# Batch 0 of an attention-and-MLP kernel: the last 64 queries taken out of the score tiles and finished inside the first GEMM, with v and w_in loaded in another order

## The chip, the core and the metric

The kernel runs on one core of a Trainium2 chip. The metric is the device time of one execution in microseconds (us), as the median of several runs. TensorE (PE) does the matrix products, ScalarE (ACT) the exponentials, the Gelus and some copies, VectorE (DVE) copies, products and divisions, GpSimd (POOL) masks, some products and the DMAs that change type, SyncE (SP) only issues DMAs.

## The reference

Eight batches of eight heads, 576 tokens and head width 64 go through causal attention with a forgetting gate; the result, with the heads side by side, is 4608 rows of 512, which go through a two-layer MLP with the exact Gelu.

```python
# q, k, v: (8, 8, 576, 64); f: (8, 8, 576); w_in: (512, 2048); w_out: (2048, 512)
cum = np.cumsum(np.log(np.clip(f, 1e-4, 1.0)), axis=-1)
scores = scale * q @ k^T + cum[:, :, :, None] - cum[:, :, None, :]
scores = np.where(causal, -1e9, scores)          # causal: key after query
x = softmax(scores) @ v                          # then (batch, token, head * 64)
out = gelu(x @ w_in) @ w_out                     # exact Gelu, by erf
```

## The kernel before

The order of all instructions on each engine is the order in which the program writes them; the engines wait for each other with semaphores that a layer adds from the tiles that are read and written. Two heads are a pair `i` (0 to 3). A part of the decay that belongs to the key is put into v as a weight: `weigh_v` multiplies v by `wT` into `vw`, whose last column holds the weight itself, so one product gives numerator and denominator; `normalize` divides.

**Batch 0** is `first_attention` (L577). `load_qk_tokens` loads q and k on POOL's queue two heads at a time. `transposes_first` turns them on PE and copies them to `qT` and `kT`, on DVE except for half of pair 0. `scores` (L279) makes the scores of a pair in four tiles of 896, 768, 896 and 640 columns for the two heads, keys on partitions, each followed by one exponential on ACT (L309). In batch 0 the mask is added by small matmuls (`key_of`, `after`). `attend` (L323) multiplies by `vw` in five blocks of 128 queries; the last block starts at query 448, so its upper 64 queries are the last 64 of the batch. `to_xT` (L356) turns x on PE in five blocks, with the copy on ACT or DVE.

The **first GEMM** (`gemm1`, L380) makes blocks of 128 of the 2048 hidden columns (`ffb` 0 to 15) for the first 512 tokens of a batch. Each block is four matmuls of 512 columns (`kt` 0 to 3, one for each pair) and then a Gelu on ACT. Batch 0 does blocks 0 to 9 in its own stage; 10 to 15 are held until batch 1. The last 64 tokens of each batch go to `tails` by `x_tail` (on POOL) and are multiplied together at the end of the kernel.

`gemm1_begin` (L662) starts the first GEMM while the last pairs are still being turned. Blocks 0 and 1 use the two `m` banks; 2 and 3 are the two halves of one `s` tile (`more`), and their Gelus come after both:

```python
        gemm1(b, 2, (2, 3), pss[2], False)
        gemm1(b, 3, range(4), pss[3], False)
        gelu(b, 2, pss[2])
        gelu(b, 3, pss[3])
```

PSUM has two tiles each of `s` (two banks), `o` and `m` (one bank each).

**Loads.** v of batch 0 comes in pieces of 128 keys by four heads: three on SP's queue (blocks 0 to 2 of the first four heads), seven on POOL's. `w_in` is four pieces of 512 hidden columns on POOL's queue, the first three right behind v, the fourth behind half of batch 1's q, k and v. POOL executes `weigh_v` for pairs 2 and 3 of batch 0 between these issues; at most eight DMAs of a queue are under way, since their semaphores are used in turn. `load_v(0, ...)` is at L154 to L159, `load_w_in` at L627 to L635.

Of the kernel before, what the change touches and what calls it, by code (L numbers as in the profile page):

```python
# [9 lines left out]
FP32 = mybir.dt.float32  # L10
# [5 lines left out]
P = 128  # L16
# [37 lines left out]
def kernel(  # L54
# [95 lines left out]
    diagonal(key_of, Alu.not_equal, 1.0, D)  # L150
    ident_bf = key_of[:, D : D + P]
    load_qk_tokens(0, 4, 6)
    nc.gpsimd.memset(v_sb[:, :, 0, 0:1], 0.0)
    load_v(0, 0, 4, ns=range(3))  # L154
    diagonal(after, Alu.is_ge, -1.0e9, D)
    load_qk_tokens(0, 6, 8)
    diagonal(ident_fp, Alu.not_equal, 1.0, 0)
    load_v(0, 0, 4, nc.gpsimd, range(3, NBLK))
    load_v(0, 4, 8, nc.gpsimd)  # L159

    qT = [consts.tile([P, S], BF16, name=f"qT{i}") for i in range(HP)]
    kT = [consts.tile([P, S], BF16, name=f"kT{i}") for i in range(HP)]
# [6 lines left out]
    def load_w_in(c):  # L169
        f4 = slice(c * d_ff // 4, (c + 1) * d_ff // 4)  # L170
        nc.gpsimd.dma_start(w_in_sb[:, :, f4], w_in_r[:, :, f4])
# [28 lines left out]
    tails = consts.tile([P, n_dm, TC], BF16)  # L200


    def transposes_first(b, i, which, pool, tag):

        src = qk_of[b][which]
        ps = pool.tile([P, JT, PT], BF16, tag=tag, name="ps_f")
        for j in range(JT):
            for h in range(2):
                nc.tensor.transpose(  # L209
                    ps[h * D : (h + 1) * D, j, :],  # L210
                    src[:, 2 * i + h, j * D : (j + 1) * D],
                    ident_bf[:PT, :PT],
                )

        dst = (qT, kT)[which][i].rearrange("d (p j) -> d p j", j=JT)
        src = ps.rearrange("d j p -> d p j")
        if b or i:
            nc.vector.tensor_copy(dst, src)  # L218
        else:
            nc.vector.tensor_copy(dst[:, 0 : PT // 2], src[:, 0 : PT // 2])  # L220
            nc.scalar.copy(dst[:, PT // 2 :], src[:, PT // 2 :])
# [55 lines left out]
    e_of = {}  # L277

    def scores(b, i, t):  # L279
        on_pe = b == 0 or (b == 1 and i == 0)  # L280
        st = s_psum.tile([P, 2, 512], FP32, tag="s", name=f"s{t}")
        c = 0
        for n, q0, w in STILES[t]:
            z = D if n == NBLK - 1 else 0
            masked = on_pe and c in SDIAG[t]
            for half in range(-1, 2 if masked else 0):
                if half == 0 and z:
                    continue
                for h in range(2):
                    d = slice(h * D, (h + 1) * D)  # L290
                    if half < 0:
                        to = st[:, h, c + z : c + w]
                        ab = kT[i][d, K0[n] : K0[n] + P], qT[i][d, q0 + z : q0 + w]
                    else:
                        last = (half + 1) * D
                        to = st[:, h, c + z : c + last]
                        c0 = (1 + h - half) * D
                        ab = key_of[d, c0 : c0 + P], after[d, c0 + z : c0 + last]
                    nc.tensor.matmul(  # L299
                        to, *ab, start=half < 0, stop=half == 1 or not masked  # L300
                    )
            c += w
        z = D if t == 1 else 0
        if z:
            et = e4[(b * HP + i) % len(e4)]
        else:
            et = e_pool.tile([P, 2, 512], BF16, tag=f"e{t}", name=f"e{t}")
        e_of[b, i, t] = et
        nc.scalar.activation(et[:, :, z:c], st[:, :, z:c], Act.Exp, scale=scale)  # L309
        for c0 in [] if on_pe else SDIAG[t]:  # L310
            nc.gpsimd.affine_select(  # L311
                out=et[:, :, c0 + z : c0 + P],
                in_=et[:, :, c0 + z : c0 + P],
                compare_op=Alu.is_ge,
                fill=0.0,
                base=z,
                pattern=[[0, 2], [1, P - z]],
                channel_multiplier=-1,
            )
# [252 lines left out]
    def behind(t, h):  # L572

        g = x_pool.tile([P, 1], FP32, tag="gate", name="gate")
        nc.gpsimd.tensor_copy(g[:PT], t[:, h, 0:1])

    def first_attention():  # L577


        def transposes(i, pool, tag):  # L580
            transposes_first(0, i, 0, pool, tag)
            transposes_first(0, i, 1, pool, tag)

        def attend_head(i, h, *at):
            attend(0, i, h, (0, 1, 2, 3, 4), *at)
            normalize(0, i, h)

        warm_up(9)
        transposes(0, o_psum, "o")
        nc.vector.tensor_tensor_scan(  # L590
            decay[:, S - 2 :: -1],
            f_sb[:, S - 1 : 0 : -1],
            none[:, 0 : S - 1],
            2.0**80,
            Alu.mult,
            Alu.add,
        )
        warm_up(2, 2 * P)
        scores(0, 0, 0)
        scores(0, 0, 1)  # L600
        transposes_first(0, 1, 0, m_psum, "m")
        scores(0, 0, 2)
        transposes_first(0, 1, 1, m_psum, "m")
        psw = o_psum.tile([P, NBLK, BH], FP32, tag="o", name="psw")
        for n in range(NBLK):
            nc.tensor.transpose(
                psw[:, n, :], decay[:, K0[n] : K0[n] + P], ident_fp[:BH, :BH]
            )
        scores(0, 0, 3)
        nc.vector.tensor_copy(wT[:, 0:4, :], psw[:, 0:4, :])  # L610
        nc.vector.tensor_copy(wT[D:P, 4, :], psw[D:P, 4, :])
        nc.vector.tensor_copy(
            vw(0)[:, :, :, D], wT[:, :, 0:H].rearrange("p n h -> p h n")
        )
        scores(0, 1, 0)
        transposes_first(0, 2, 0, m_psum, "m")
        scores(0, 1, 1)
        transposes_first(0, 2, 1, m_psum, "m")
        scores(0, 1, 2)
        scores(0, 1, 3)  # L620
        transposes_first(0, 3, 0, m_psum, "m")
        scores(0, 2, 0)
        transposes_first(0, 3, 1, m_psum, "m")
        weigh_v(0, 0, nc.vector, 0, NBLK - 1)
        weigh_v(0, 0, nc.vector, NBLK - 1)
        weigh_v(0, 1, nc.vector)
        load_w_in(0)  # L627
        load_w_in(1)
        load_w_in(2)
        weigh_v(0, 2)  # L630
        weigh_v(0, 3)
        load_qk_tokens(1, 0, 4)
        nc.gpsimd.memset(v_sb[:, :, 0, 0:1], 0.0)
        load_v(1, 0, 4, nc.gpsimd)
        load_w_in(3)  # L635
        load_qk_tokens(1, 4, 8)
        load_v(1, 4, 8, nc.gpsimd)
        scores(0, 2, 1)
        scores(0, 2, 2)
        scores(0, 2, 3)  # L640
        for ms in ((0, 1, 2, 3), (4,)):
            for h in range(2):
                attend(0, 0, h, ms)
        for h in range(2):
            normalize(0, 0, h)
        scores(0, 3, 0)
        scores(0, 3, 1)
        for h in range(2):
            attend_head(1, h, m_psum, "m")
        scores(0, 3, 2)  # L650
        scores(0, 3, 3)
        for h in range(2):
            attend_head(2, h)
        to_xT(0, 0, nc.scalar.copy)
        to_xT(0, 1, nc.scalar.copy)
        attend_head(3, 0)
        attend_head(3, 1)
        both = s_psum.tile([P, 2, 1024], BF16, tag="s", name="ps_x2")
        to_xT(0, 2, nc.scalar.copy, ps=both[:, 0, 0:XC])
        gemm1_begin(0, both)  # L660

    def gemm1_begin(b, both):  # L662

# [141 lines left out]
    for b in range(B):  # L805
        if b == 0:
            first_attention()
        elif b == 1:
            second_attention()
        else:  # L810
            attention(b)
        if b == 0:
            x_tail(0)
        for ffb in range(4 if b < 2 else 5, n_ff):
            if b == 0 and ffb in HELD:
                continue
            aside = ffb in (7, 8) if b > 1 else b == 1 and ffb % 4 < 2
            gemm1(b, ffb, ps=spare() if aside else None)
            if b == 1 and ffb % 2 == 0:
                at = HELD[(ffb - 4) // 2]  # L820
                gelu(0, at, h_of[at])
            if b == 0:
                if ffb == 7:
                    weigh_v(1, 0)
                    load_w_out(0)
                    weigh_v(1, 1)
                    load_w_out(1)
                    load_qk_tokens(2)
                if ffb == 8:
                    for which in range(2):  # L830
                        transposes_first(1, 0, which, o_psum, "o")
            elif b + 1 < B:
                first, gap = (5, 3) if b == 1 else (1, 4)
                at, late = divmod(ffb - first, gap)
                if late == 0:
                    untangle(b + 1, at)
                if late == gap - 2 and (b > 1 or at < 2):
                    weigh_v(b + 1, at)
                if ffb == (9 if b == 1 else 14):
                    load_qk_tokens(b + 2)  # L840
# [34 lines left out]
```

## Time and profile before

| what | value |
| --- | --- |
| median of 3 runs (lowest, highest) | 336.46 us (335.54, 336.92) |
| the profiled execution, its time | 335.98 us |
| its span, from first to last instruction | 334.1 us |
| granted TensorE clock | 0.999 |
| PE busy | 325.7 us, 97% |
| ACT busy | 206.7 us, 62% |
| first matmul of the first GEMM of batch 0 | 22.89 us |
| first scores of batch 1 | 33.18 us |

Times within the profile are us from the start of the span. In a timeline line the columns are start, length, engine, line, operation, out<-in, shape and count; in brackets stand the idle time of the engine before it and who ended it. In a group line the first number after the bar is busy time, then the mean ns of one instruction, then idle time before them and its releasers. Matmuls are pipelined, so the length of a matmul's line includes its way through the array.

### The profile page before, as it was taken

How to read it: one execution, taken by the hardware profiler on the slowest of the kernel's cores; microseconds unless marked ns; L12 is line 12 of the kernel's file. 1: busy time of each engine (PE TensorE's matmuls, PEld its weight loads, DVE VectorE, ACT ScalarE, POOL GpSimd, SP SyncE). 2: the span in 40 equal slices, each digit the busy share in tenths (PEclk: the TensorE clock that was granted, in tenths of full speed). 3: DMA queues.
4: the chain of work that ended last, by engine and by line, in shares of the span. 5: the costliest groups of instructions: out<-in, count | busy, mean ns of one | idle time of the engine just before them, and what ended most of it. 6: DMA issues, size and time to landing. Idle time of an engine off the chain costs nothing.

```text
span 334.1 us, 7820 instructions
## 1 busy us (share of the span) xinstructions
PE 325.7 (97%) x3161; PEld 170.7 (51%) x3161; DVE 183.9 (55%) x424; ACT 206.7 (62%) x299; POOL 133.3 (40%) x260
## 2 busy tenths in 40 slices
PE   7899999999999999999999999999999999999995
PEld 3674555445554466445644565455544654444443
DVE  5761657754549754894589447954795450010011
ACT  3976886974536786578736892788278836404600
POOL 8897873066336044704453355334432420000000
PEclk9999999999999999999999999999999999999999
DMA  8999999959999699489939894969700520021013
GB/s 120 206 191 217 197 193 137 206 94 239 190 198 178 106 216 145 103 132 192 190 103 139 169 200 124 141 119 200 175 0 2 100 76 33 0 77 51 0 43 83
DMA packets 97427, 44.16 MB, mean 132 GB/s; under 512 B 75728, under 2 KB 92368, under 8 KB 97392
## 3 DMA queue, kind: packets, MB, share of 16 engines
q1 hardware_dynamic: 79344, 27.55, 42.7%
q0 software_dynamic: 17648, 15.60, 30.0%
q8 instruction: 24, 0.39, 0.5%
q10 hardware_dynamic: 400, 0.52, 0.4%
q14 instruction: 11, 0.09, 0.1%
HBM read 36.85 MB, written 9.44 MB: 139 GB/s over the span
## 4 chain that ended last, share of the span: by engine, by line
PE 91%; DMA 3%; ACT 2%; DVE 1%; issue 1%; ACTq 0%
PE ps L385 36%; PE ps L489 26%; PE o L330 9%; PE ps L429 8%; PE s L299 8%; DMA xT<-x 3%; ACT e L309 2%; PE ps_w L196 1%; PE ps_f L209 1%; PE ps L549 1%; PE ps L525 1%; PE ps_x L363 1%; DVE x L344 0%; DVE r L343 0%; DVE qT L218 0%
## 5 line engine op out<-in xcount | busy, mean ns | idle before, releaser
L405 ACT ACTIVATE g<-ps 128x512 bf16<-128x512 f32 x138 | 78.5, 601 | 79.8 <-PE ps L385 79.3
L385 PE MATMUL ps<-xT,w_in_sb 128*128 128x512 bf16 x512 | 113.7, 379 | 0.5 <-DMA xT<-x 0.5
L309 ACT ACTIVATE e<-s 128x896 bf16<-128x896 f32 (+2 forms) x128 | 100.0, 836 | 22.3 <-PE s L299 19.5
L489 PE MATMUL ps<-w_out_sb,g 64*128 64x512 bf16 (+1 forms) x711 | 108.1, 377 | 0.0
L385 PEld LDWEIGHTS <-w_in_sb 128*128 128x128 bf16 x576 | 55.6, 98 | 68.0 <-issue 3.6
L311 POOL TENSOR_SCALAR_AFFINE_SELECT e<-e 128x256 bf16<-128x256 bf16 (+1 forms) x135 | 49.4, 385 | 91.9 <-ACT e L309 91.6
L489 PEld LDWEIGHTS <-g 64*128 64x128 bf16 (+1 forms) x711 | 39.4, 95 | 34.7 <-issue 4.2
L268 POOL TENSOR_TENSOR vw<-v_sb,wT 128x640 bf16<-128x640 f32 x30 | 38.6, 1290 | 24.7 <-PE ps L549 13.9
L299 PE MATMUL s<-qT,kT 64*128 64x320 bf16 (+4 forms) x384 | 43.1, 276 | 2.4 <-ACT e L309 1.5
L249 DVE COPY qT<-tq 64x288 bf16<-64x288 bf16 x96 | 41.7, 434 | 3.6 <-DMA tq<-q 2.2
L249 DVE COPY kT<-tk 64x288 bf16<-64x288 bf16 x96 | 40.8, 425 | 1.6
L497 DVE COPY ot<-ps 128x512 f32<-128x512 f32 x20 | 13.8, 692 | 47.0 <-PE ps L489 47.0
L330 PEld LDWEIGHTS <-e 128*128 128x128 bf16 x960 | 34.5, 98 | 8.7 <-POOL e L311 2.9
L330 PE MATMUL o<-vw,e 128*128 128x65 bf16 x960 | 37.0, 194 | 0.3 <-issue 0.3
L438 DVE COPY ot<-ps 128x512 f32<-128x512 f32 (+2 forms) x9 | 5.7, 633 | 50.0 <-PE ps L429 50.0
L344 DVE TENSOR_TENSOR x<-o,r 128x320 bf16<-128x320 f32 x64 | 31.5, 492 | 2.9 <-DVE r L343 0.7
L299 PEld LDWEIGHTS <-kT 64*128 64x128 bf16 x384 | 19.5, 94 | 22.7 <-issue 6.1
L429 PE MATMUL ps<-w_out_sb,g 128*128 128x512 bf16 (+2 forms) x144 | 28.0, 355 | 0.0
L429 PEld LDWEIGHTS <-g 128*128 128x128 bf16 x144 | 13.4, 97 | 14.5
L343 DVE RECIPROCAL r<-o 128x5 f32<-128x5 f32 x64 | 12.1, 188 | 10.6 <-PE o L330 10.5
L509 DVE TENSOR_TENSOR ot<-ot,ps 128x512 f32<-128x512 f32 x22 | 15.1, 685 | 1.1
L385 PE MATMUL ps<-tails,w_in_sb 128*128 128x512 bf16 x64 | 14.3, 378 | 0.0
(69 smaller groups left out, 154.1 us busy)
## 6 DMA issues: line engine op xcount, KB each, us to landing
out_dram<-ot SPq DMA_DIRECT2D x32, 256.0 KB, 2.6
v_sb<-in_v_dram SPq DMA_DIRECT2D x24, 256.0 KB, 4.8
q<-in_q_dram POOLq DMA_DIRECT2D x6, 576.0 KB, 6.3
k<-in_k_dram POOLq DMA_DIRECT2D x6, 576.0 KB, 8.3
w_in_sb<-in_moe_w_in_dram POOLq DMA_DIRECT2D x4, 512.0 KB, 8.1
w_out_sb<-in_moe_w_out_dram POOLq DMA_DIRECT2D x4, 512.0 KB, 7.9
v_sb<-in_v_dram POOLq DMA_DIRECT2D x13, 128.0 KB, 7.2
v_sb<-in_v_dram SPq DMA_DIRECT2D x9, 128.0 KB, 4.8
```

What stands on the lines that cost most here:

```text
L249: nc.vector.tensor_copy(rows[:, odd], src[odd * D : (odd + 1) * D, 2 * i + h].rearrange("d j p -> d p j"),)
L268: eng.tensor_tensor(vw(b)[:, hs, n0:n1, 0:D], v_sb[:, hs, n0:n1, :], w.unsqueeze(3).to_broadcast([P, 2, n1 - n0, D]), Alu.mult,)
L299: nc.tensor.matmul(to, *ab, start=half < 0, stop=half == 1 or not masked)
L309: nc.scalar.activation(et[:, :, z:c], st[:, :, z:c], Act.Exp, scale=scale)
L311: nc.gpsimd.affine_select(out=et[:, :, c0 + z : c0 + P], in_=et[:, :, c0 + z : c0 + P], compare_op=Alu.is_ge, fill=0.0, base=z, pattern=[[ ...
L330: nc.tensor.matmul(o[:, m, :], e_of[b, i, t][:, h, c : c + P], vw_of[b][:, 2 * i + h, n, :], start=(n == 0), stop=(n == m),)
L344: nc.vector.tensor_tensor(x_of[b, i][:, :, h, :], o[:, :, 0:D], r.unsqueeze(2).to_broadcast([P, NBLK, D]), Alu.mult,)
L385: nc.tensor.matmul(ps, w_in_sb[:, kt, ffb * P : (ffb + 1) * P], src[:, kt, 0:TC], start=(kt == 0), stop=(kt == n_dm - 1),)
L405: nc.scalar.activation(g_of[c][ffb], ps, Act.Gelu)
L429: nc.tensor.matmul(pss[ts][:, c0:c1], g_of[c][kt][:, ts * P : (ts + 1) * P], w_out_sb[:, kt, c0:c1], start=(kt == 0), stop=(kt == n_ff - 1),)
L489: nc.tensor.matmul(banks[r], g_of[c][kt][rows, ts * P : (ts + 1) * P], w_out_sb[rows, kt, :], start=kt == (steps.index("r") if r else 0), ...
L509: nc.vector.tensor_tensor(ot, ot, bank, Alu.add)
```

## The change

It concerns batch 0 alone.

1. The score tiles of batch 0 hold only queries 0 to 511 and are up to 1024 columns wide for the two heads: `scores_a` (key block 0), `scores_b` (key blocks 1 and 3), `scores_c` (key block 2 of two pairs). The scores of queries 512 to 575 are made by `scores_t` (key blocks 0 to 3 of two pairs, in eight parts of 64 queries) and `scores_t4` (the last 64 keys, all four pairs).
2. The attention of the first 512 queries is four blocks (`attend_0`), with four transposes (`to_xT_0`). The last 64 queries are multiplied by `attend_tail` between blocks 4 and 5 of the first GEMM, and turned and copied straight to `tails` on DVE by `tail_0` between blocks 5 and 6. `x_tail(0)` on POOL is gone.
3. `gemm1_begin` is not used for batch 0. Blocks 0 to 3 are all begun with `kt` 0 and 1, then `scores_t(2)` puts the tail scores of pairs 2 and 3 into two `o` banks, with two exponentials of 512 columns; then `kt` 2 and 3 follow for the four blocks, each with its Gelu when it is summed.
4. All of batch 0's v is issued by SP, in eight pieces of 128 keys by four heads, behind a memset that POOL does after its three selects, and one piece for the last 64 keys of all heads. POOL reads one element of the fourth piece (`gate`) before it issues `w_in` 0 and 1. `w_in` 2 comes after `weigh_v` of pairs 2 and 3 (now on POOL without the last keys); the last keys of all heads are weighed by one product on POOL, behind the first half of batch 1's q and k.
5. The copy of pair 1's k is split in two.

```diff
-    nc.gpsimd.memset(v_sb[:, :, 0, 0:1], 0.0)
-    load_v(0, 0, 4, ns=range(3))
     diagonal(after, Alu.is_ge, -1.0e9, D)
     load_qk_tokens(0, 6, 8)
     diagonal(ident_fp, Alu.not_equal, 1.0, 0)
-    load_v(0, 0, 4, nc.gpsimd, range(3, NBLK))
-    load_v(0, 4, 8, nc.gpsimd)
+    nc.gpsimd.memset(v_sb[:, :, 0, 0:1], 0.0)
+    load_v(0, 0, 4, ns=range(4))
+    load_v(0, 4, 8, ns=range(4))
...
+    def scores_a(i):
+        scores_0([(i, 0, 0, TC)], new_e(0))
+
+    def scores_b(i):
+        scores_0([(i, 1, P, TC - P), (i, 3, 3 * P, P)], new_e(2))
+
+    def scores_c(i):
+        scores_0([(i, 2, 2 * P, 2 * P), (i + 1, 2, 2 * P, 2 * P)], new_e(3))
+
+    def scores_t(i, banks=None):
+        parts = [(ii, n, TC, TL) for ii in (i, i + 1) for n in range(NBLK - 1)]
+        scores_0(parts, new_e(3), banks)
+
+    def scores_t4():
+        scores_0([(i, NBLK - 1, TC, TL) for i in range(HP)], e4[0][:, :, D:])
...
+    def attend_tail():
+        o = o_psum.tile([P, NBLK, D + 1], FP32, tag="o", name="o")
+        for i in range(HP):
+            for n in range(NBLK):
+                e, c = e0_of[i, n, True]
+                for h in range(2):
+                    nc.tensor.matmul(
+                        o[h * D : (h + 1) * D, i, :],
+                        e[:, h, c + TC : c + S],
+                        vw_of[0][:, 2 * i + h, n, :],
+                        start=(n == 0),
+                        stop=(n == NBLK - 1),
+                    )
+        x = x_pool.tile([P, NBLK, 2, D], BF16, tag="x", name="x")
+        x_of[0, "tail"] = x.rearrange("p n h d -> p (n h) d")[:, 0:HP]
+        divide(x_of[0, "tail"], o, HP)
...
+        scores_b(2)
+        weigh_v(0, 0, nc.vector, 0, MAIN)
+        weigh_v(0, 1, nc.vector, 0, MAIN)
+        g = x_pool.tile([P, 1], FP32, tag="gate", name="gate")
+        nc.gpsimd.tensor_copy(g, v_sb[:, 3, MAIN - 1, 0:1])
         load_w_in(0)
         load_w_in(1)
+        weigh_v(0, 2, n1=MAIN)
+        weigh_v(0, 3, n1=MAIN)
+        nc.gpsimd.memset(v_sb[D:P, :, MAIN, 0:1], 0.0)
+        load_v(0, ns=[MAIN])
         load_w_in(2)
-        weigh_v(0, 2)
-        weigh_v(0, 3)
         load_qk_tokens(1, 0, 4)
+        nc.gpsimd.tensor_tensor(
+            vw(0)[:, :, MAIN, 0:D],
+            v_sb[:, :, MAIN, :],
+            wT[:, MAIN, 0:H].unsqueeze(2).to_broadcast([P, H, D]),
+            Alu.mult,
+        )
...
+        scores_a(3)
+        attend_0(0, o_psum, "o")
+        scores_b(3)
+        scores_c(2)
+        attend_0(1, m_psum, "m")
+        to_xT_0(0, nc.scalar.copy)
+        scores_t(0)
+        attend_0(2, o_psum, "o")
+        to_xT_0(1, nc.scalar.copy)
+        scores_t4()
+        attend_0(3, o_psum, "o")
+
+        pss = [gemm1(0, ffb, (0, 1)) for ffb in range(2)]
         both = s_psum.tile([P, 2, 1024], BF16, tag="s", name="ps_x2")
-        to_xT(0, 2, nc.scalar.copy, ps=both[:, 0, 0:XC])
-        gemm1_begin(0, both)
+        to_xT_0(2, nc.scalar.copy, both[:, 0, 0:TC])
+        more = s_psum.tile([P, 2, 512], FP32, tag="s", name="ps1")
+        pss += [more[:, 0, :], more[:, 1, :]]
+        gemm1(0, 2, (0, 1), pss[2])
+        to_xT_0(3, nc.vector.tensor_copy, both[:, 1, 0:TC])
+        gemm1(0, 3, (0, 1), pss[3])
+        scores_t(2, [o_psum.tile([P, TC], FP32, tag="o", name="s0") for _ in range(2)])
+        for kt in (2, 3):
+            for ffb in range(4):
+                gemm1(0, ffb, (kt,), pss[ffb])
...
             if b == 0:
+                if ffb == 4:
+                    attend_tail()
+                if ffb == 5:
+                    tail_0()
```

## The prediction

> **What bounds the kernel now.** I read the engine shares and the chain of waits first, then the timelines of TensorE (PE) and ScalarE (ACT) up to 33 us, the groups by shape, and the DMA windows.
>
> ```profile
> PE 325.7 (97%) x3161; PEld 170.7 (51%) x3161; DVE 183.9 (55%) x424; ACT 206.7 (62%) x299; POOL 133.3 (40%) x260
> ...
> PE 91%; DMA 3%; ACT 2%; DVE 1%; issue 1%; ACTq 0%
> ```
>
> PE is busy for 97% of the span and carries 91% of the chain. Once it has reached batch 1 it does not rest, so the change is worth what it does to the moment when PE finishes the last first-GEMM block of batch 0 (ffb 9, after the transposes at 31.21). From there I let everything slide rigidly.
>
> ```profile
> 7.63 9.31 ACT L309 ACTIVATE e<-s 128x896 bf16<-128x896 f32 x12 [0.44 <-PE s L299]
> 17.55 3.15 ACT L309 ACTIVATE e<-s 128x896 bf16<-128x896 f32 x4 [0.60 <-PE s L299]
> ...
> 23.09 0.69 ACT L366 COPY xT<-ps_x 128x640 bf16<-128x640 bf16 x1 [0.82 <-PE ps_x L363]
> 23.80 1.28 ACT L405 ACT_TABLE_LOAD   x1
> 25.39 1.08 ACT L405 ACTIVATE g<-ps 128x512 bf16<-128x512 f32 x2 [0.30 <-PE ps L385]
> 26.90 1.57 ACT L405 ACTIVATE g<-ps 128x512 bf16<-128x512 f32 x3 [0.43 <-PE ps L385]
> ```
>
> ACT has no gap from 7.63 to 16.94: its sixteen exponentials pace the attention. Then it loads the Gelu table while PE is in the first GEMM; the first Gelu waits for PE (0.30), not PE for it.
>
> ```profile
> 21.10 0.80 PE L330 MATMUL o<-vw,e 128*128 128x65 bf16 x18
> 22.23 0.54 PE L330 MATMUL o<-vw,e 128*128 128x65 bf16 x12 [0.34 <-issue]
> 22.62 0.44 PE L363 MATMUL ps_x<-key_of,x 128*128 128x128 bf16 x5
> 22.89 1.03 PE L385 MATMUL ps<-xT,w_in_sb 128*128 128x512 bf16 x4
> 23.84 0.44 PE L363 MATMUL ps_x<-key_of,x 128*128 128x128 bf16 x5
> 24.11 7.17 PE L385 MATMUL ps<-xT,w_in_sb 128*128 128x512 bf16 x32
> 31.21 0.45 PE L209 MATMUL ps_f<-key_of,q 96*64 96x96 bf16 x12
> ```
>
> The first GEMM starts at 22.89. Of the 32 matmuls from 24.11 on (0.22 each), twelve end blocks 0 to 3, so block 4 starts at 24.11 + 12 x 0.22 = 26.75. There is no idle time in it. These two marks are what I follow.
>
> ```profile
> L309 ACT ACTIVATE e<-s 128x896 bf16<-128x896 f32 x64 | 58.7, 918 | 19.9 <-PE s L299 17.6
> L309 ACT ACTIVATE e<-s 128x768 bf16<-128x768 f32 x32 | 25.7, 804 | 1.2 <-PE s L299 1.0
> L309 ACT ACTIVATE e<-s 128x640 bf16<-128x640 f32 x32 | 22.5, 704 | 1.3 <-PE s L299 0.9
> ```
>
> From 640 to 896 columns is 214 ns, 0.836 ns a column, so 1024 columns should take 1.025 us; back to back they overlap by 0.1 (twelve of them in 9.31), so one costs 0.925.
>
> **Score tiles and the ACT chain.** The elements are the same (12,800 per partition before and after); 16 exponentials become 14, which saves two fixed parts of about 0.07 us. The tails are the gain: only ten 1024-wide exponentials and one tail tile (pairs 0, 1) stand ahead of the first GEMM's inputs. The first needs fewer keys and starts at about 7.3, the next at 8.2. The third waits for pair 1's k: DVE is in its scan until 8.02, then copies q (0.76) and the first half of k (0.46), plus scores 0.3, so 9.75, a gap of 0.6. Five steps of 0.925 later, at 14.4, the eighth begins (pair 3's first tile). The ninth stands behind pair 0's attention on PE (20 matmuls at 1.06/30 = 0.035, 0.7 us), which waits for weighted v until 14.3: a gap of 0.3. It starts at 15.7, and the tenth, `scores_c(2)`, ends at 17.6.
>
> **v on SyncE, w_in gated.** SyncE's first v piece waits for the memset, now behind the `ident_fp` select (it ended at 8.1; the memset was at 5.8), and nothing but v queues on SyncE. Before, the first half of v landed by 15.0 and the second by 16.9 (issues at 8.85 and 12.44, landing 6.2 and 4.5 later in the DMA windows). Pieces of 256-byte rows from SyncE went alone as follows (window 64 to 65 us):
>
> ```profile
> q1 hardware_dynamic: 1030, 0.26, 114.7%
> ```
>
> 0.26 MB a us is 0.5 us a piece; later windows give 0.6. From 10.4 the fourth lands at about 13.5. The gate then lets GpSimd issue w_in(0) at 13.8 against 13.38 and w_in(1) at 14.5 against 14.80: 18.7 for the first piece at the earlier pace (19.4 before), ahead of its use. Behind the gate on GpSimd queue w_in(0..1), `weigh_v` 2 and 3, w_in(2), q and k of batch 1; behind the wait for the ninth piece queue v of batch 1 and w_in(3). w_in(3) landed 8.65 after 25.14, at 33.8, for block 12 at 36.9; it may be 3 us late for nothing. `weigh_v` 2 waits for the eighth piece: 17.0 by 0.6 a piece with some sharing, plus 1.29 x 512/640 = 1.03, so pair 2's attention starts at 18.1 and not 17.7.
>
> **To the first GEMM.** From 18.1: attention 2 0.7, `to_xT_0(1)` 0.22, tail scores of the last block 0.35, attention 3 0.7 with 0.3 for an o bank that DVE must divide first. GEMM start 20.4 against 22.89: 2.5 us won, and 40 of 120 attention matmuls and four transposes are gone from here.
>
> **Inside the first GEMM.** Four matmuls 0.86, transposes 0.22, two matmuls 0.43, 0.4 waiting for pair 3's division, transposes 0.22, two matmuls 0.43, sixteen tail scores at about 0.022 = 0.36: the scores of `scores_t(2)` are done at 23.4. That is a new ACT step ahead of the table load. Then ACT does two 512-wide exponentials (1.1 after 0.2 of latency), the load (1.28) and three Gelus (0.60 + 2 x 0.50), so block 2's Gelu ends 4.1 later, at 27.5. PE has seven matmuls (1.5 us) for that time. Then it stops: blocks 2 and 3 are halves of one s tile, and in the built list of waits block 3's last matmul waits for exactly the Activation count that block 2's Gelu raises. Before, these two blocks put their Gelus off until both were summed. PE idles about 2.6 us; one matmul later, at 27.8, block 4 starts: 1.05 later than 26.75. All that was won is lost here.
>
> The load's row is 1.28 us, and at 33.53 the same load is followed by an activation at 34.83, within 0.02 us. [...]
>
> **Tail work.** Blocks 4 to 9 now hold 40 matmuls and 8 transposes. The nearest row with 64-wide weights is the twelve q transposes in 0.28 us (7.72 to the next step, two column halves side by side): 0.023 each, so 0.9 + 0.2, with 0.1 for the division: 1.2. The upper bound is the full-width 0.035: 1.7. Below, 0.9 if the division hides. [...] The copies to `tails` move from GpSimd (0.44 at 33.25, off the path) to DVE, idle from 24.9 to 31.7: nothing, or 0.5 on DVE if that cover were gone.
>
> **Sum.** +1.05 + 1.2 = +2.25, and 0.25 for v's second half (below), +2.5. The profiled execution took 335.98 with a span of 334.1; 338.5 for it. The median is 336.46, 0.48 higher: 339.0.
>
> **Rivals.**
> - Not slower: PE reaches the tail scores sooner. If the gaps that I put in (0.6 for k, 0.3 for v, 0.4 for `weigh_v`, 0.7 for banks and divisions) close by more than half, they end at 22.2 and all of the Gelu wait moves with them: -0.15 + 1.2, +1.0, 337.5. The point is 22.8. For it: ACT alone would allow 21.2. Against it: three of the gaps are waits that the built list has. With every gap closed and the tail at 0.9 it is still -0.2, so faster needs the Gelu wait not to act as read. Within 0.5%: 0.17; faster: 0.04.
> - Slower still: the eighth v piece is not in when w_in's packets start. From 59 to 60 us SyncE's queue (q1) ran beside a weight load (q0):
>
> ```profile
> q0 software_dynamic: 157, 0.16, 93.7%
> q1 hardware_dynamic: 152, 0.04, 29.4%
> ```
>
> It got 152 packets in that us, against 858 alone from 66 to 67, so a leftover piece of 512 packets takes 3.4 us and not 0.6. `weigh_v` 2, pair 2's attention and the GEMM then slide by 1 to 3 us: 340 to 342. Chance 0.21.
> - The gate does nothing (w_in issued as before, v as slow): 339 to 340, inside the range; the forecast itself 0.58.
>
> **Numbers.** 0.5% is 1.7 us, about what a measurement of this kernel can tell from no change. Slower 0.79, same 0.17, faster 0.04. The range goes from the first rival's 337.5 to the middle of the second: 337.5 to 341.2.
>
> **What would show it.** PE's first GEMM matmul near 20.4; a PE gap of 2 to 3 us released by ACT's Gelu just before block 4; two 512-wide exponentials right ahead of the table load; ffb 9 ending 2 to 3 us later. I am wrong if that gap is under 1 us, if the GEMM starts under 19.5 or over 22, or if the shift at batch 1 does not reach the end.

## The result, and the profile after

Twelve runs of the changed kernel gave a median of 339.18 us (337.33 to 342.26), twelve of the kernel before beside them 335.52 (334.85 to 336.92). The ratio is 1.0111, with a 95% interval of 1.0078 to 1.0145: slower by 3.7 us. The forecast put 2.5 us on the time of before.

The profiled execution took 342.26 us with a span of 340.6, the slowest of the twelve, so I read it together with the profiles of the variants. First its page: the shares, the granted clock in 40 slices, and the chain.

```profile
PE 329.0 (97%) x3189; PEld 171.9 (50%) x3189; DVE 185.0 (54%) x427; ACT 206.6 (61%) x297; POOL 129.2 (38%) x255
...
PEclk9699899999999999999999999999999999999999
...
PE 91%; DMA 3%; DVE 2%; ACT 2%; issue 1%; POOL 0%; DVEq 0%; POOLq 0%
```

PE still carries 91% of the chain. The loss lies before batch 1: its first scores start at 40.40 instead of 33.18 (+7.2), and the last output store is 6.4 later. The clock row has a 6 and an 8 near the front. The table of windows shows these two stretches (columns: window, its length, busy time of PE, PEld, DVE, ACT and POOL with the instructions in brackets, then granted clock, DMA share, GB/s):

```profile
8.50:15.30 6.80, 6.80 (x101) 4.76 (x97) 4.40 (x9) 4.09 (x4) 1.38 (x3) 0.50 1.04 202
32.40:35.80 3.40, 3.40 (x53) 1.88 (x54) 0.61 (x2) 0.91 (x2) 3.40 (x6) 0.50 1.19 193
```

PE ran at half clock (0.50 in both rows) for 6.83 us from 8.47 and for 3.41 us from 32.36. In the profile of before there is no such stretch until 333.6. PE's timeline of after (start, busy time, line, operation, and in brackets the idle time ahead with what ended it):

```profile
7.96 0.45 PE L208 MATMUL ps_f<-key_of,q 96*64 96x96 bf16 x12 [0.70 <-DMA q<-in_q_dram]
...
18.13 0.79 PE L640 MATMUL o<-vw,e 128*128 128x65 bf16 x20 [1.00 <-DVE vw L269]
...
24.02 1.02 PE L386 MATMUL ps<-xT,w_in_sb 128*128 128x512 bf16 x4
...
27.03 1.69 PE L386 MATMUL ps<-xT,w_in_sb 128*128 128x512 bf16 x7
31.15 1.24 PE L386 MATMUL ps<-xT,w_in_sb 128*128 128x512 bf16 x5 [2.44 <-ACT g L406]
32.32 1.31 PE L676 MATMUL o<-vw,e 128*64 128x65 bf16 x40
```

In this execution the first GEMM (24.02) is even later than before (22.89): half clock and a late product of v stand ahead of it. Then seven matmuls, and PE stands for 2.44 us until ACT has done a Gelu. On ACT, that is:

```profile
27.13 1.08 ACT L613 ACTIVATE e<-s 128x512 bf16<-128x512 f32 x2 [1.24 <-PE s L604]
28.23 1.28 ACT L406 ACT_TABLE_LOAD   x1
29.52 1.57 ACT L406 ACTIVATE g<-ps 128x512 bf16<-128x512 f32 x3
```

Two 512-wide exponentials, the table load, three Gelus: 4.0 us from the tail scores on, as in the forecast, and PE has 1.5 us of work for that time. The third thing stands in GpSimd's timeline:

```profile
19.29 0.81 POOL L170 DMA_DIRECT2D w_in_sb<-in_moe_w_in_dram  x1
20.09 0.69 POOL L109 DMA_DIRECT2D q<-in_q_dram  x1
20.76 0.68 POOL L109 DMA_DIRECT2D k<-in_k_dram  x1
24.99 1.04 POOL L751 TENSOR_TENSOR vw<-v_sb,wT 128x512 bf16<-128x512 f32 x1 [3.55 <-DVE x L654]
...
26.38 3.68 POOL L121 DMA_DIRECT2D v_sb<-in_v_dram  x5 [0.30 <-POOL v_sb L757]
```

GpSimd rests for 3.55 us ahead of the product of the ninth v piece. The row names a division on VectorE that ended at 24.92 and of which the product reads nothing; what it waited for is the piece itself, which was issued on SyncE at 19.18 and landed at 24.82 (in e1 the row names it). Batch 1's v is issued at 26.38 instead of 21.37 behind it, and its k of heads 4 to 7 at 31.44 instead of 28.98.

### The profile page after: what moved, and what is told of

Same layout as the page of the kernel before. It is cut to its first block, busy times and chain, and to the rows that moved or that the text cites. A ratio compares the mean times of both kernels' runs of the same rounds, so it can differ in the third digit from the quotient of the medians.

```text
span 340.6 us, 7870 instructions
## 1 busy us (share of the span) xinstructions
PE 329.0 (97%) x3189; PEld 171.9 (50%) x3189; DVE 185.0 (54%) x427; ACT 206.6 (61%) x297; POOL 129.2 (38%) x255
## 3 DMA queue, kind: packets, MB, share of 16 engines
HBM read 36.85 MB, written 9.44 MB: 136 GB/s over the span
## 4 chain that ended last, share of the span: by engine, by line
PE 91%; DMA 3%; DVE 2%; ACT 2%; issue 1%; POOL 0%; DVEq 0%; POOLq 0%
PE ps L386 36%; PE ps L490 26%; PE ps L430 8%; PE o L331 8%; PE s L300 7%; PE ps_f L208 2%; DMA q<-in_q_dram 2%; PE s L604 1%; DMA xT<-x 1%; PE ps L550 1%; DVE vw L269 1%; PE ps L526 1%; PE o L640 0%; ACT g L406 0%; ACT e L310 0%
## 5 line engine op out<-in xcount | busy, mean ns | idle before, releaser
L386 PE MATMUL ps<-xT,w_in_sb 128*128 128x512 bf16 x512 | 115.1, 381 | 2.5 <-ACT g L406 2.4
L310 ACT ACTIVATE e<-s 128x896 bf16<-128x896 f32 x112 | 87.7, 836 | 21.0 <-PE s L300 17.4
L269 POOL TENSOR_TENSOR vw<-v_sb,wT 128x640 bf16<-128x640 f32 (+1 forms) x30 | 38.7, 1292 | 21.4 <-DMA v_sb<-in_v_dram 11.5
L250 DVE COPY kT<-tk 64x288 bf16<-64x288 bf16 x96 | 41.8, 435 | 1.6
L250 DVE COPY qT<-tq 64x288 bf16<-64x288 bf16 x96 | 40.2, 419 | 1.4
L300 PE MATMUL s<-qT,kT 64*128 64x256 bf16 (+1 forms) x336 | 37.0, 276 | 0.5 <-DVE kT L219 0.3
L331 PEld LDWEIGHTS <-e 128*128 128x128 bf16 x840 | 30.3, 98 | 7.9 <-POOL e L312 2.5
L331 PE MATMUL o<-vw,e 128*128 128x65 bf16 x840 | 32.3, 194 | 0.0
L345 DVE TENSOR_TENSOR x<-o,r 128x320 bf16<-128x320 f32 x56 | 27.5, 492 | 1.9
L300 PEld LDWEIGHTS <-kT 64*128 64x128 bf16 x336 | 16.6, 94 | 19.2 <-issue 3.7
L430 PEld LDWEIGHTS <-g 128*128 128x128 bf16 x144 | 13.5, 98 | 14.5
L344 DVE RECIPROCAL r<-o 128x5 f32<-128x5 f32 x56 | 10.5, 188 | 9.1 <-PE o L331 9.1
L386 PE MATMUL ps<-tails,w_in_sb 128*128 128x512 bf16 x64 | 14.3, 377 | 0.0
```

What stands on the lines that cost most here:

```text
L250: nc.vector.tensor_copy(rows[:, odd], src[odd * D : (odd + 1) * D, 2 * i + h].rearrange("d j p -> d p j"),)
L269: eng.tensor_tensor(vw(b)[:, hs, n0:n1, 0:D], v_sb[:, hs, n0:n1, :], w.unsqueeze(3).to_broadcast([P, 2, n1 - n0, D]), Alu.mult,)
L300: nc.tensor.matmul(to, *ab, start=half < 0, stop=half == 1 or not masked)
L331: nc.tensor.matmul(o[:, m, :], e_of[b, i, t][:, h, c : c + P], vw_of[b][:, 2 * i + h, n, :], start=(n == 0), stop=(n == m),)
L345: nc.vector.tensor_tensor(x_of[b, i][:, :, h, :], o[:, :, 0:D], r.unsqueeze(2).to_broadcast([P, NBLK, D]), Alu.mult,)
L386: nc.tensor.matmul(ps, w_in_sb[:, kt, ffb * P : (ffb + 1) * P], src[:, kt, 0:TC], start=(kt == 0), stop=(kt == n_dm - 1),)
```

## The experiments

Theory at the start: the wait for block 2's Gelu and the tail work are the cost, as forecast. Rivals: the clock (half speed after PE's waits), the overlap of v products on VectorE and GpSimd, and the late issues on GpSimd. "Table-load delta" below is how much later than in before's profile ACT loads its exponential table for batch 1 (33.53 there): it sums up all that happened in batch 0.

**e1: the changed kernel once more, without an edit,** for a second profile of it.

> The changed kernel once more, unaltered. Theory A (the order on PE and ACT sets the time): block 4 of the first GEMM again waits 2.4 to 2.6 us for block 2's Gelu, and the time stands 2 to 3 us over the kernel before. Theory C (the granted clock adds to it): runs with the mean clock at 0.997 or more come out 2 to 3 us over the kernel before, runs below 0.996 come out 3 to 6 over, and the profile shows the half-speed stretches at another place or not at all.

Measured: 339.03 us (six runs, ratio 1.0105 [1.0079, 1.0130]); this profile took 339.11. GEMM at 20.90, no half clock before it, VectorE's two products 0.69 us each, the Gelu wait again 2.44, block 4 at 28.25. A half-clock stretch from 28.7 to 32.1 follows the wait. The ninth piece landed at 26.75, and GpSimd's row now names it:

```profile
26.92 1.04 POOL L751 TENSOR_TENSOR vw<-v_sb,wT 128x512 bf16<-128x512 f32 x1 [5.68 <-DMA v_sb<-in_v_dram]
```

So the Gelu wait and the late piece belong to the kernel; the late GEMM of the first profile belongs to that execution.

**e2: all four Gelus after both sums.**

```diff
-                gemm1(0, ffb, (kt,), pss[ffb])
+                gemm1(0, ffb, (kt,), pss[ffb], False)
+        for ffb in range(4):
+            gelu(0, ffb, pss[ffb])
```

> The Gelus of blocks 0 to 3 are put off until all four blocks are summed; nothing else. Theory A: PE no longer waits for block 2's Gelu inside block 3, but block 4 needs the bank that block 0's Gelu frees, which ends 3.1 us after the tail scores instead of 4.1: PE still idles about 1.4 us, and 0.9 to 1.2 us are won against the changed kernel (337.8 to 338.3). Rival (the time is set further up, by v and the clock): within 0.4 us of the changed kernel.

Measured: 339.28 us (1.0109 [1.0086, 1.0132]). The wait ahead of block 4 fell from 2.44 to 1.25, as the edit should do, and batch 1's first scores came at +1.7. But there PE waited 1.33 us for batch 1's k, and the delta grew to 3.1 and then 4.4. The gain was taken back by a wait that I had not forecast.

**e3: e2, and block 4 in a spare bank,** so that no Gelu has to be done first.

```diff
             aside = ffb in (7, 8) if b > 1 else b == 1 and ffb % 4 < 2
+            aside = aside or (b == 0 and ffb == 4)
...
-                if ffb == 5:
+                if ffb == 6:
                     tail_0()
```

> As the one with the late Gelus, and block 4 is put into an o bank, so that it waits for no Gelu; the transposes of the tail come one block later. Theory A: the wait of 2.4 us before block 4 is gone and at most 0.5 us of it comes back at a later bank: 2 to 2.4 us won against the changed kernel, 336.8 to 337.2. If PE's idle stretch is also what drops the clock, 0.5 to 1.5 us more and a narrower spread. Rival (set further up): under 0.8 us won.

Measured: 338.48 us (1.0084 [1.0054, 1.0113]). No wait is left ahead of block 4 (26.30), the delta is +0.77, and yet only 0.7 us of the 2.4 comes out at the end, and as the intervals overlap it may be less. PE's timeline shows the new wait:

```profile
27.25 0.83 PE L676 MATMUL o<-vw,e 128*64 128x65 bf16 x40
...
38.63 0.45 PE L208 MATMUL ps_f<-key_of,q 96*64 96x96 bf16 x12
41.21 0.45 PE L208 MATMUL ps_f<-key_of,k 96*64 96x96 bf16 x12 [2.13 <-DMA k<-in_k_dram]
```

The k of heads 4 to 7 was issued at 32.72 and landed at 41.17 (before: 28.98 and 36.85). The wait is followed by a half-clock stretch from 41.8 to 45.2.

**e4: GpSimd's first product behind VectorE's second.**

```diff
+        g2 = x_pool.tile([P, 1], FP32, tag="gate", name="gate")
+        nc.gpsimd.tensor_copy(g2, vw(0)[:, 3, 0, 0:1])
         weigh_v(0, 2, n1=MAIN)
```

> GpSimd reads one element of what DVE's second product of v and weights writes, before it starts its own two products, so that the two engines' products no longer run at once; nothing else. Theory B (the two block each other at SBUF): DVE's two products take 0.68 us each instead of 1.5, pair 0's attention starts 0.8 to 1.6 us earlier, and the time falls by as much: 337.6 to 338.4. Rival (DVE's products are slow for another reason, or something later is late anyway): DVE's rows stay at 1.5 us, or the time stays within 0.4 us of the changed kernel.

Measured: 339.49 us (1.0106 [1.0078, 1.0134]), no change: the overlap of products is not the cause (in e1's profile there was none either). Its profile, the fastest of its six runs (337.08) and without a half-clock stretch ahead of 334, is the forecast in plain: GEMM at 20.48, delta +2.25.

```profile
27.61 1.24 PE L386 MATMUL ps<-xT,w_in_sb 128*128 128x512 bf16 x5 [2.44 <-ACT g L406]
28.78 0.83 PE L676 MATMUL o<-vw,e 128*64 128x65 bf16 x40
...
30.52 0.31 PE L692 MATMUL ps_x<-key_of,x 64*64 64x64 bf16 x8
```

**e5: e3, and the ninth piece's product behind batch 1's loads on GpSimd.** In `first_attention` the `tensor_tensor` on `MAIN` was moved behind the loads of `w_in(3)`, q, k and v (all but v's own last block).

> As e3 (Gelus of blocks 2 and 3 after both are summed, block 4 in a spare bank, tail transposes one block later), and on GpSimd the product of the ninth v piece is put behind the loads of batch 1's q, k and v, so that these no longer queue behind its wait. My theory: e3 turned the Gelu wait into a wait for batch 1's k, which lands late (38.7 against 36.9) because its issue stands behind that product. Then the PE wait of 2.1 us near 41 is gone, batch 1's scores stay about 0.8 us behind the kernel before, and the time is 335.5 to 336.5. Rival A (the k transfer is late because the DMA engines are full, whatever the order of issues): a PE wait over 1 us for k stays near 41, and the time stays at 338 to 339. Rival B (half-speed stretches of the clock are what costs): a half-speed stretch appears all the same, with 337 or more.

Measured: 346.0 us (1.0302 [1.0264, 1.0339]), a miss by 10 us. The reason stands in GpSimd's timeline:

```profile
27.82 0.69 POOL L109 DMA_DIRECT2D q<-in_q_dram  x1 [2.09 <-DMA w_in_sb<-in_moe_w_in_dram]
30.73 0.67 POOL L109 DMA_DIRECT2D k<-in_k_dram  x1 [2.21 <-DMA q<-in_q_dram]
32.54 2.99 POOL L121 DMA_DIRECT2D v_sb<-in_v_dram  x4 [1.14 <-DMA k<-in_k_dram]
35.54 1.06 POOL L756 TENSOR_TENSOR vw<-v_sb,wT 128x512 bf16<-128x512 f32 x1
```

Each of the three waits ends 0.28 us after the landing of the eighth issue before it on GpSimd's queue (`w_in(2)` at 27.54, q at 30.45, k at 32.26), since eight semaphores are used in turn. A product behind eleven issues ends at 36.6, and `attend_tail`, which PE began at 27.15, stood on it for 9.19 us from 27.5. (The k of e3 landed at 41.17, not at the 38.7 of the expectation.) The run says nothing on the theory; it says that the product must come ahead of the loads and its data earlier, which is e10.

**e6: v, `w_in` and the products in the order of the kernel before,** with the new score tiles and the tail (three v pieces on SyncE, the rest on GpSimd, no gate, no ninth piece: the lines of the diff for v and `w_in` undone).

> The score tiles and the tail as in the changed kernel, but v, w_in and the v products in the order of the kernel before (three v pieces on SyncE, the rest on GpSimd, no gate, no ninth piece). My theory (the Gelu wait and the tail work are the cost, and the v order only moves the start of the GEMM): a Gelu wait of 2.4 us is still ahead of block 4, block 4 starts at 27.5 to 28.5, batch 1's k lands near 36.9, and the time is 337.5 to 339. Rival (the v order is what costs, through late issues on GpSimd): the time falls to that of the kernel before, 335.5 to 336.5. Second rival (the v order is what lets the shorter chain of exponentials pay): the GEMM starts after 22 and the time is above 339.5.

Measured: 339.57 us (1.0111 [1.0072, 1.0151]). GEMM at 20.86, Gelu wait 2.44, block 4 at 28.20, delta +2.6, no wait for k. The new order of v and `w_in` is neither what makes the GEMM early nor, with the Gelu wait in place, what costs.

**e7: matmuls on zeros in two of PE's waits,** to hold the clock.

```diff
         scores_a(0)
+        warm_up(3)
         transposes(1, 0)
...
+                if (kt, ffb) == (3, 3):
+                    fill = o_psum.tile([P, TC], FP32, tag="o", name="ps_w")
+                    for _ in range(10):
+                        nc.tensor.matmul(fill, warm[:, 0:P], warm, start=True, stop=True)
                 gemm1(0, ffb, (kt,), pss[ffb])
```

> The changed kernel with matmuls on zeros put into two PE waits: three of 512 columns (0.65 us) ahead of pair 1's q transposes, and ten (2.2 us) ahead of block 3's last matmul, where PE waits for block 2's Gelu. Theory of the clock (PE's waits drop the granted clock to half for 3.41 us, which costs up to 1.7 us more than the wait itself, in some runs): no half-speed stretch before 40 us, times spread less, median 337.0 to 338.0. Rival (the half-speed stretches are not due to these waits, or hide in later waits): half-speed stretches as before, median 338.8 to 339.5; where fillers run past the end of the wait, up to 0.3 slower.

Measured: 339.23 us (1.0099 [1.0061, 1.0137]), no faster. The clock did rise: five of six runs have a mean granted clock of 0.997 or more, against eight of eighteen of the unedited kernel. The profiled execution (340.14, its slowest) has no half-clock stretch, but its ninth piece landed at 28.56, k at 43.38, and PE waited 0.46 and 1.27 us for batch 1's q and k. The clock alone does not bring the time back here.

**e8: e6 with the edits of e3.**

> e6 with e3's edits: score split and tail as changed, v in the order of the kernel before, no Gelu wait ahead of block 4. My theory: neither the Gelu wait nor the wait for k; block 4 at 25.5 to 26.5, tail work 1.2, batch 1's first scores 0 to 1 us behind the kernel before, time 335.0 to 336.5. Rival (a wait for batch 1's data or a half-speed stretch takes the place of the Gelu wait here too): a PE wait over 1 us near 41, 337.5 to 339.

Measured: 335.85 us (twelve runs, 1.0014 [0.9989, 1.0038]): as before. Neither the Gelu wait nor the wait for k is left. With e3 (338.48) and e6 (339.57) this closes the square: taking away the Gelu wait is worth 0.7 us with v in the new order (339.18 to 338.48) and 3.7 with v in the old. Of these 3.7 the two profiles show 2.3 (the deltas are +2.62 and +0.30); the rest lies in executions of e6 that were not profiled. Three of these five have a mean granted clock under 0.997, but one at 1.000 took 339.71, so the clock is not all of it, and what else it is stays open.

**e9: the changed kernel, its ninth v piece issued right behind the other eight.**

```diff
     load_v(0, 4, 8, ns=range(4))
+    load_v(0, ns=[NBLK - 1])
...
-        nc.gpsimd.memset(v_sb[D:P, :, MAIN, 0:1], 0.0)
-        load_v(0, ns=[MAIN])
```

> The changed kernel, with the ninth v piece (the last 64 keys of all heads) issued on SyncE right behind the other eight, no longer behind GpSimd's products. Theory: the piece lands late (25 to 29 us) because it goes beside w_in's packets, and GpSimd's queue, with batch 1's loads in it, stands behind it; issued early it lands by 18.5, batch 1's first v load is issued by 22.5, k of heads 4 to 7 lands near 37. The Gelu wait of 2.4 us ahead of block 4 stays, so batch 1 is 2.2 to 4 us behind the kernel before: 338.0 to 339.0. Rival (the late loads are nearly all of the loss): 336.5 or less. Rival (early, it delays w_in and the GEMM): GEMM start after 22, above 339.5.

Measured: 338.62 us (1.0094 [1.0066, 1.0122]). The piece landed at 17.4, k at 38.3; the Gelu wait of 2.44 stayed. In its profile (337.46) the delta is +2.46.

**e10: e9 with the edits of e3.**

> e9 with e3's edits, so that neither the Gelu wait nor the late loads are left. Theory (two floors, each hiding behind the other: PE's Gelu wait, and GpSimd's late loads): no wait before block 4 above 0.5 us, no wait for k near 41, batch 1's first scores 0.3 to 1 us behind the kernel before, 335.3 to 336.5, against 338.5 for e3. Rival (w_in comes later, since the ninth piece goes ahead of it, or another queue is late): a new PE wait over 1 us in 20 to 45, above 337.

Measured: 335.72 us (1.0005 [0.9981, 1.0030]), against 338.48 for e3, which differs only in when the ninth piece is issued. GpSimd's timeline, to be read against that of after:

```profile
20.16 0.68 POOL L109 DMA_DIRECT2D k<-in_k_dram  x1
20.84 1.06 POOL L750 TENSOR_TENSOR vw<-v_sb,wT 128x512 bf16<-128x512 f32 x1
...
22.25 3.68 POOL L121 DMA_DIRECT2D v_sb<-in_v_dram  x5 [0.29 <-POOL v_sb L756]
```

The product waits for nothing, v of batch 1 goes 4.1 us earlier, k lands at 38.15, and PE no longer waits for it, to be read against the last line of e3:

```profile
38.57 0.45 PE L209 MATMUL ps_f<-key_of,q 96*64 96x96 bf16 x12
38.84 0.42 PE L209 MATMUL ps_f<-key_of,k 96*64 96x96 bf16 x12
```

The first GEMM waited 0.48 us for `w_in` (0.31 in e3), less than the rival's 1 us.

**e11: e10 with e4's edit.**

> e10 with e4's edit as well (GpSimd's first v product behind VectorE's second). Theory: where the two pairs of products would overlap, the overlap is gone; elsewhere GpSimd's start moves by up to 0.3 us and the GEMM with it. 335.0 to 336.3, within 0.5 of e10. Rival (the overlap is what makes the first GEMM late in most runs): 1 us under e10, 334.5, faster than the kernel before.

Measured: 336.08 us (1.0008 [0.9986, 1.0030]), not to be told from e10. No version beats the kernel before.

**e12: e8 without the tail attention.**

> e8 (v as before, free banks) without the tail attention: the 40 matmuls, the division and the 8 transposes are left out, and a memset of the tails' columns stands in for them. It prices the tail work at the end of the kernel. Theory (everything from batch 1 on slides rigidly): e8's 335.85 less 1.2 (0.85 for the matmuls, 0.3 for the transposes), 334.5 to 335.0. Rival (a later wait, for k or weights of batch 1, swallows it): 335.5 or more.

Measured: 335.95 us (1.0008 [0.9986, 1.0030]), where I expected 334.5 to 335.0. The rival was right that something swallows it, though it is neither k nor weights. PE of e12:

```profile
24.16 2.76 PE L387 MATMUL ps<-xT,w_in_sb 128*128 128x512 bf16 x12
27.31 1.89 PE L387 MATMUL ps<-xT,w_in_sb 128*128 128x512 bf16 x8 [0.38 <-ACT g L407]
29.75 1.89 PE L387 MATMUL ps<-xT,w_in_sb 128*128 128x512 bf16 x7 [0.56 <-ACT g L407]
```

and ACT of e8, with the tail in it:

```profile
24.20 1.08 ACT L614 ACTIVATE e<-s 128x512 bf16<-128x512 f32 x2 [1.24 <-PE s L605]
25.30 1.28 ACT L407 ACT_TABLE_LOAD   x1
26.59 3.54 ACT L407 ACTIVATE g<-ps 128x512 bf16<-128x512 f32 x7
```

ACT runs without a rest from the tail's exponentials to the seventh Gelu at 30.1. Before, the table load started at 23.80; here, with a GEMM that starts 1.8 us earlier (21.09), it starts at 25.30. Leave the tail's matmuls out, and PE waits 0.94 us for Gelus in their place: ACT stands right behind PE. In e8 itself PE waits for no Gelu. From the start of the GEMM to batch 1's first scores it needs 12.4 us instead of 10.3: 1.1 for the tail's matmuls and transposes, 0.3 for the tail scores of pairs 2 and 3, the rest for one more set of transposes and two short waits. So e8 only draws level because PE has that much more to do behind an earlier start, and leaving 1.1 of it out wins nothing because ACT then holds PE. That the tail's two exponentials ahead of the load are what makes ACT late is argued, not shown; whether they would do better behind the Gelus, at the price of one more table load, was not tried.

## Why the prediction was right, and where it was not

**The sum, step by step.** The executions without a half-clock stretch ahead of batch 1 and without a wait for k (profiles of e4, e9 and e6) follow the forecast's steps. They are each the fastest or second fastest of their kernel (337.08, 337.46 and 338.12 us).

- GEMM start: forecast 20.4; 20.48, 20.69, 20.86, and 20.90 in e1. The working of score tiles, v and ACT holds to 0.1 to 0.5 us, whether v comes in the new order or the old. A 1024-wide exponential cost 0.92, as taken. What is late is v: its fourth piece landed at 14.0 to 14.4 (e4, e9, e1) instead of 13.5, so pair 0's attention began at 14.9 to 15.3 instead of 14.3 and pair 2's at 18.4 to 18.8 instead of 18.1.
- The Gelu wait: forecast 2.6; 2.44 in every profile that keeps the order of the change, and gone in e3. Block 4: forecast 27.8; 27.83, 28.04, 28.20. It is the dependence of one matmul on the other half of its tile, as the forecast named it.
- Tail work: forecast 1.2; 0.83 + 0.31 = 1.14 in e4. The 40 matmuls took 0.021 each, near the 0.023 of the q transposes (whose 0.28 us is that from 31.21 to 31.49; at 7.72 the next step is 0.88 later). The 40 weight loads have a mean of 111 ns, 4.4 us one after the other, but took 0.72 us in all, so they ran side by side (in the profile of after, at half clock, 156 ns and 1.2 us).
- The table load: forecast 1.28, and 1.28 in the profile of after. It began 0.02 us behind the last exponential (27.13 + 1.08, then 28.23) and the Gelu 0.01 us behind the load (28.23 + 1.28, then 29.52).
- The shift at batch 1: forecast +2.5; +2.25, +2.46 and +2.6. The 0.25 for v's second half that stands in the sum has no working, and no run shows it: the eighth piece landed at 16.2 to 16.5, ahead of the 17.0 assumed.
- Slips in the working that moved nothing: the row of 1030 packets is that of 63 to 64 us (64 to 65 has 917); the terms of the third exponential add up to 9.54, not 9.75 (it began at 9.83 in e1); twelve exponentials in 9.31 us overlap by 0.07, not 0.1; the middle of 340 to 342 is 341.0, not 341.2.

**What the sum left out, first: batch 1's q and k.** In listing what queues on GpSimd behind the wait for the ninth piece I named v of batch 1 and w_in(3), and not `load_qk_tokens(1, 4, 8)`, which stands right behind them. I also priced v's second half and took the ninth piece for free. It landed 5.6 to 9.7 us after its issue, beside `w_in`'s packets, against 3.0 to 3.6 when it was issued ahead of them (e9 to e11). The rival of a starved piece had the right mechanism on the wrong piece: the eighth landed at 16.5 (e1), in time, and the ninth starved, for longer than the 3.4 us that this rival gave a piece. With the Gelu wait in place PE comes to batch 1 late enough to hide most of it: e9 is 0.6 us below the changed kernel, and their intervals overlap. With the Gelu wait gone it is worth 2.8 us (e3 against e10). Two costs stood in parallel, and removing either alone shows little.

**Second: the clock.** The forecast was +2.5 on the time of before, a ratio of 1.0075, and that is just outside the measured interval. The runs split by clock: over the changed kernel, e1 and e4 together, the nine runs with a mean granted clock of 0.997 or more have a median of 337.9, 2.4 above before; the other fifteen have 339.8. Of the 63 runs of before beside the variants, 60 are at 0.997 or more. In the profiles one half-clock stretch can be priced: e1 and e4 run the same work from block 4 on, which starts 0.42 apart, and the deltas at the table load are 4.17 and 2.25; so 3.41 us at half speed cost 4.17 - 2.25 - 0.42 = 1.5. That it is PE's waits which bring the stretches is supported by where they lie, in steps of 3.413 us that the last section shows, and by e7's higher clocks; that taking them away lowers the time was not shown, since in e7's profile late data took their place.

**Third: the slide to the end is not rigid.** Of the shift at batch 1, 1.3 (e4), 1.6 (e9) and 2.0 (e6) reached the last store; 0.6 to 1.0 was won back on the way. I had carried all of it. This error and the clock work against each other in the total, and the kernel before ran 0.9 us under the median that I started from; 339.0 and 339.18 lie closer than the steps behind them. In these three executions the forecast's own steps brought 1.3 to 2.0 us to the end, a third to a half of the 3.7 between the medians; the rest is what the forecast did not have, the clock and the late data as far as the runs show. The mechanism was right as far as it went, and that the total agrees to 0.2 us is luck.

**The rivals.** "Not slower" needed the tail scores by 22.8 and the gaps to close; they did not (the tail scores of e1 ended near 23.9). "The gate does nothing" is out: `w_in` was issued only after the gate, at 14.11, and with the gate undone (e6) the GEMM started at the same time, so it does what it says and buys nothing here.

## What to carry to other kernels

Before pricing a stage that starts earlier, follow every engine that it hands work to: here the score split put two exponentials ahead of a table load, and ACT's run of Gelus took back on its side what PE had won on its own. For each wait that is added to a queue that also issues transfers, write down every instruction behind it up to the next point where the queue is idle, and look a stage further for who uses them. And when one repair brings too little, look for the wait that has moved into its place, and try the repairs together before dropping either.

## What the runs showed of the hardware

- Half-clock stretches came in multiples of 3.41 us: 6.83 and 3.41 in the changed kernel, 3.41 in e1 and e3, 10.24 in e5. That of e5 began at 30.9, 3.4 us into its wait of 9.19; the others began 0.5 to 1.2 us after PE had gone on from a wait of 0.70 to 2.44. A wait of 2.44 us brought one in two profiles (the changed kernel, e1) and none in three (e4, e6 and e9, with mean granted clocks of 0.998, 1.000 and 0.998). Where the wait lies tells them apart. In the profile of the changed kernel the starts of the stretches, that at the end of the span included, are whole multiples of 3.413 us apart (8.47, 32.36 and 339.56: 7 and 90 of them). With each of these profiles cut into steps of 3.413 us from such a start, 2.20 us (changed kernel) and 2.44 us (e1) of the wait of 2.44 lay within one step, and the stretch began where that step ended; in e4, e6 and e9 a step's end cut the wait, with 1.91, 1.54 and 1.51 us in the fuller step. In e3 it was 2.13 us of the wait for k, in the step that ended at 41.8, where the stretch began. In the profiles of before and after, from 5 us on, the three steps with 2.20 us or more without a matmul were followed by half clock (2.20 from 28.95 and 2.88 from 336.15 in after, 3.40 from 330.22 in before), and none with 1.36 or less was, but for one: that of 5.06 to 8.47 in the changed kernel, with 1.1 us idle and small matmuls otherwise. That PE's idle time within a step decides is my estimate from these figures, and the step from 5.06 speaks against it.
- VectorE and GpSimd were slower in the v products when both were at them. In the profile of after they overlapped, and two products on VectorE took 3.03 us, two on GpSimd 2.52; alone they took 1.30 (e1) and 2.08 (e3). The pairs took 3.07 together against 3.38 in sum. Where the two engines meet, at SBUF as Theory B of e4 had it or elsewhere, no run shows.
- GpSimd's issue of a DMA waited for the eighth issue before it to land: 2.09, 2.21 and 1.14 us ahead of single issues in e5 (each wait ended 0.28 us after that landing), 2.04 in e10. This comes from the eight semaphores that the program uses in turn; how many transfers the queue itself would hold, no run shows.
